# GpSimd's elementwise work of an attention and two-MoE kernel put on VectorE, and the ELU in another form

## The chip, the cores and the metric

One core of one Trainium2 chip runs the whole program. The metric is the device time in microseconds of one execution; three executions of the kernel before were timed. TensorE (PE), VectorE (DVE), ScalarE (ACT), GpSimd (POOL) and SyncE (SP, which issues the DMAs here) each work through a queue of their own in order.

## What is computed

Attention whose keys and values are means over 8 neighbouring positions, then an MoE with ELU, then a second MoE with a softmax-gated unit and a normalization. Everything is float32 in and out; 4608 tokens of 512 numbers.

```python
k_p = k.reshape(B, H, Sp, 8, D).mean(axis=3)          # v_p likewise; B, H, S, D = 8, 8, 576, 64
attn = softmax(scale * q @ k_p.T)                     # sums + 1e-9
x = (attn @ v_p) -> (4608, 512)
h = x @ w_in                                          # 512 -> 2048
g = np.where(h > 0, h, np.exp(np.minimum(h, 0)) - 1)  # ELU
x = g @ w_out                                         # 2048 -> 512
h = x @ w_in2                                         # 512 -> 1024
solu = h * softmax(h)
out = ((solu - mean) / sqrt(var + 1e-6) * g_ln) @ w_out2
```

## The kernel before

A float32 product is made of three fp32r products (high x high, high x low, low x high), so every operand is split: ScalarE casts the high part, VectorE or GpSimd subtracts it for the low part. Tokens come in 9 blocks of 512.

**Direct stage** (to about 410 us; blocks j = 0, 1, 2). For each block and each f of 16 column blocks of 128 hidden units, `m_h1` runs 12 matmuls into a PSUM bank `h` and ScalarE makes `e`; `m_elu` makes the ELU on VectorE and ScalarE's cast `gh`; `m_glo` the low part `gl_`; `m_o1` 12 matmuls into four banks `o`. Attention of later tokens runs in between, in pieces (`att_half`): scores on TensorE (L173), maximum and subtraction on VectorE (L189, L198), exponent on ScalarE (L203), sum on VectorE (L212 to L214), the division `es` on GpSimd (L216), transposes (L228, L233) with ScalarE copies `a`, products with v (L252) and copies `xr`, `xh`. `w_out_split` makes the high and low parts of w_out: `woh` on ScalarE, `wol` on GpSimd (L452).

While blocks 1 and 2 run, `combo_in` and `combo_out` prepare weight combinations for the rest: for each of 8 pairs of column blocks, `ci` (from w_in) and `co` (from w_out), each by `combos`: four subtractions of 128x256 (L469), two casts of 128x512 on ScalarE (L474), two low-part subtractions (L479), and DMAs to the DRAM tensors `w1d` and `w3d`. One generator hands these steps out, 2.6 of them per half column block.

**Paired stage** (about 412 to 961 us; three rounds of two blocks). Two blocks and the two halves of features form a 2x2 product that is done with seven products instead of eight (P1, P2, V, S2, S3, A22, S4). `h_step` runs the seven products of hidden pair k over combined operands, adds them up with `keep` (ScalarE copies a bank to `sp`, L670) and VectorE adds (L703, L714, L722), and applies `elu` to the four quarters `g` (11, 12, 21, 22) in SBUF. The quarter 21 comes straight from a bank (argument `h`, L680 to L682), the others from SBUF (`h` is None, L676 to L678). `g_sum` forms sums of quarters in place, 128x1024 each: V, S3 and S4 on GpSimd, S2 on VectorE (L736). `g_op` splits them (cast `op` L742, low part L743) for `mul_o`, which runs the second seven products against the streamed `wr` tiles. Attention for later blocks goes on in the first two rounds; in the last, `prep_in` prepares the second MoE's weights (L391 to L394, L422, L428, L429).

**MoE 2** (from 961 us) is TensorE work in a fixed rhythm: products x, y, z (L832), transposes (L904), products po (L919).

Most of the program isn't issued in the order written: a scheduler orders each engine's queue by its own cost estimates and the data dependences (only the start is under `manual_schedule`). So a change of engine also moves neighbouring instructions.

Of the kernel before, what the change touches and what calls it, by code (L numbers as in the profile page):

```python
# [9 lines left out]
F32R = mybir.dt.float32r  # L10
# [3 lines left out]
AF = mybir.ActivationFunctionType  # L14
ALU = mybir.AluOpType
# [4 lines left out]
def kernel(  # L20
# [15 lines left out]
    nc = tc.nc  # L36
# [428 lines left out]
    def combos(b11, b12, b21, b22, t, w, d):  # L465

        t1, t2, t3, t4 = (t[:, i] for i in range(4))
        for o, x, y in ((t1, b12, b11), (t3, b22, b12), (t2, b22, t1), (t4, b21, t2)):
            nc.gpsimd.tensor_tensor(o, x, y, op=ALU.subtract)  # L469
            yield  # L470
        tf = t.rearrange("p s a f -> p (s a f)")
        for m in range(2):
            c = slice(512 * m, 512 * m + 512)
            nc.scalar.copy(w.bitcast(F32R)[:, c], tf[:, c])  # L474
            yield
        for m in range(2):
            c = slice(512 * m, 512 * m + 512)
            eng = nc.vector if m else nc.gpsimd
            eng.tensor_tensor(tf.bitcast(F32R)[:, c], tf[:, c], w[:, c], op=ALU.subtract)  # L479
            yield  # L480
        for hl, z in enumerate((w, tf)):
            nc.sync.dma_start(out=d[hl], in_=z.rearrange("p (s f) -> p s f", s=4))
        yield
# [39 lines left out]
    def m_h1(j, f):  # L523
        n = sizes[j]
        g, fo = f // 4, (f % 4) * P
        h = ps.tile([P, 512], F32, name="h1", tag="B")
# [5 lines left out]
                )  # L532
                i += 1
        e = p1.tile([P, 512], F32, name="e", tag="e")
        if j == 0:

            nc.scalar.activation(e[:, 0:n], h[:, 0:n], AF.Relu, scale=-1.0)
            nc.scalar.activation(e[:, 0:n], e[:, 0:n], AF.Exp, scale=-1.0)
        else:
            nc.scalar.activation(e[:, 0:n], h[:, 0:n], AF.Exp)  # L540
        gt[j, f] = (e, h)

    def m_elu(j, f):
        n = sizes[j]
        e, h = gt[j, f]
        if j == 0:
            nc.vector.scalar_tensor_tensor(  # L547
                e[:, 0:n], e[:, 0:n], 1.0, h[:, 0:n], op0=ALU.subtract, op1=ALU.max
            )
        else:  # L550
            nc.vector.tensor_scalar(e[:, 0:n], e[:, 0:n], 1.0, 1.0, op0=ALU.min, op1=ALU.subtract)
            nc.vector.tensor_tensor(e[:, 0:n], e[:, 0:n], h[:, 0:n], op=ALU.max)
        gh = p1.tile([P, 512], F32R, name="gh", tag="gh")
        nc.scalar.copy(gh[:, 0:n], e[:, 0:n])  # L554
        gt[j, f] = (e, gh)
# [116 lines left out]

    def elu(d, h=None):
        e = pq.tile([P, 512], F32, name="ep", tag="ep", bufs=2)
        if h is None:
            nc.scalar.activation(e, d, AF.Exp)  # L676
            nc.vector.tensor_scalar(e, e, 1.0, 1.0, op0=ALU.min, op1=ALU.subtract)
            nc.vector.tensor_tensor(d, e, d, op=ALU.max)  # L678
        else:
            nc.scalar.activation(e, h, AF.Relu, scale=-1.0)  # L680
            nc.scalar.activation(e, e, AF.Exp, scale=-1.0)
            nc.vector.scalar_tensor_tensor(d, e, 1.0, h, op0=ALU.subtract, op1=ALU.max)  # L682

    hx = {}

# [40 lines left out]
    GQ = {"P1": 11, "P2": 12, "V": 21, "S2": 21, "S3": 11, "A22": 22, "S4": 12}  # L726

    def g_sum(n, t):
        d, x, y, op, eng = {
            "V": (21, 21, 22, ALU.add, nc.gpsimd),  # L730
            "S2": (21, 21, 11, ALU.subtract, nc.vector),
            "S3": (11, 22, 21, ALU.subtract, nc.gpsimd),
            "S4": (12, 12, 21, ALU.subtract, nc.gpsimd),
        }[n]
        d, x, y = (gslot(q, 2 * t, 2) for q in (d, x, y))
        eng.tensor_tensor(d, x, y, op=op)  # L736

    def g_op(s, t):
        n = ORDER[s]
# [558 lines left out]
```

## Time and profile before

| | us |
|---|---|
| median of the times (1375.02 to 1377.74) | 1376.96 |
| the profiled execution | 1375.29 |
| its span, first to last instruction | 1373.5 |
| PE busy in the span | 1290.4 (94%) |
| DVE busy | 1020.6 (74%) |
| ACT busy | 725.6 (53%) |
| POOL busy | 365.4 (27%) |

The span is that of one execution under the profiler. A share of busy time is a mean over stages with different limits, so it is read stage by stage: where TensorE is busy all the time at clock 1.00, nothing that another engine does costs time; where it isn't, its waits name what came last, and that engine's queue shows what stood ahead. The granted clock is a share of full speed (2.4 GHz). Matmuls overlap one another, so their pace is read from the distance of their starts and not from their durations.

### The profile page before, as it was taken

Reading aid. Unit: us, or ns where it says so; the run is one execution under the profiler, and the core shown is the slowest. Engines: PE = TensorE matmul, PEld = TensorE weight load, DVE = VectorE, ACT = ScalarE, POOL = GpSimd, SP = SyncE. Lnnn points to the kernel's source line nnn. Section 1 sums busy time; section 2 is a strip of 40 time slices with the busy share of each in tenths; the row PEclk is TensorE's granted clock in tenths of the full one; section 3 lists DMA queues with packets and bytes.
Section 4 is the critical chain, followed back from the end, with each engine's and each line's share of the span. In section 5 each row is a group of like instructions: output and inputs, shape, how many; then the busy total and the mean of one; then the engine's idle time right before and its main releaser. Section 6 shows DMA issues by size and latency. Waiting matters only on the chain.

```text
span 1373.5 us, 17423 instructions
## 1 busy us (share of the span) xinstructions
PE 1290.4 (94%) x5972; PEld 1023.6 (75%) x5972; DVE 1020.6 (74%) x1517; ACT 725.6 (53%) x1266; POOL 365.4 (27%) x266
## 2 busy tenths in 40 slices
PE   5889988899999999999999999899999999999998
PEld 4667766677876787777887767778788888888887
DVE  7888785776676889849799488996766666757573
ACT  4778553455454574445564346633545554545453
POOL 3546766752220216301126000170000000000000
PEclk8999998999999999999999999999999999999999
DMA  8588476683338775787765778899311011101001
GB/s 261 175 247 255 141 234 194 208 274 115 95 97 295 229 228 181 237 275 211 215 188 198 261 238 266 289 349 343 115 54 54 24 54 54 54 25 53 31 17 39
DMA packets 143273, 236.06 MB, mean 172 GB/s; under 512 B 13520, under 2 KB 61136, under 8 KB 141776
## 3 DMA queue, kind: packets, MB, share of 16 engines
q1 hardware_dynamic: 143184, 234.93, 53.1%
q8 instruction: 48, 0.79, 0.2%
q14 instruction: 41, 0.34, 0.1%
HBM read 168.82 MB, written 66.06 MB: 171 GB/s over the span
## 4 chain that ended last, share of the span: by engine, by line
PE 44%; DVE 8%; DMA 4%; ACT 2%; issue 1%; SPq 0%; POOL 0%; POOLq 0%; ACTq 0%; DVEq 0%
PE po L919 14%; PE oA L752 8%; PE x L832 7%; PE hA L658 5%; PE z L832 3%; DVE op L743 3%; PE pt L904 2%; PE y L832 2%; DMA raw<-in_w 2%; DMA x1d<-xo 1%; PE oB L752 1%; DMA wr<-w3d 1%; DVE g L736 1%; PE xyz L832 1%; DMA su<-x0d 1%
## 5 line engine op out<-in xcount | busy, mean ns | idle before, releaser
L752 PE MATMUL oA<-op,wr 128*128 128x512 f32 x864 | 206.5, 397 | 3.9 <-DMA wr<-w3d 3.3
L919 PE MATMUL po<-w,dhl 128*128 128x512 f32 x864 | 208.5, 394 | 0.9 <-ACT dhl L907 0.9
L752 PEld LDWEIGHTS oA<-op,wr 128*128 128x128 f32 x864 | 163.4, 191 | 43.8 <-issue 5.9
L919 PEld LDWEIGHTS po<-w,dhl 128*128 128x128 f32 x864 | 160.9, 188 | 35.4 <-ACT dhl L907 1.3
L736 POOL TENSOR_TENSOR g<-g,g 128x1024 f32<-128x1024 f32 x36 | 109.0, 3046 | 279.3 <-DVE g L682 231.2
L743 DVE TENSOR_TENSOR op<-g,op 128x1024 fp32r<-128x1024 f32 x84 | 136.9, 1654 | 21.1 <-ACT op L742 20.9
L742 ACT CAST op<-g 128x1024 fp32r<-128x1024 f32 x84 | 87.3, 1051 | 86.6 <-PE oA L752 40.0
L894 POOL TENSOR_TENSOR sc<-sc,mhalf 128x1 f32<-128x1 f32 x36 | 23.3, 646 | 402.5 <-DVE sc L893 327.2
L658 PE MATMUL hA<-sS,wr 128*128 128x512 f32 x432 | 111.7, 397 | 6.1 <-ACT sp L670 4.0
L452 POOL TENSOR_TENSOR wol<-wo,woh 128x512 fp32r<-128x512 f32 x48 | 72.9, 1519 | 108.1 <-ACT woh L451 108.0
L658 PEld LDWEIGHTS hA<-sS,wr 128*128 128x128 f32 x432 | 79.8, 189 | 28.8 <-ACT sp L670 6.9
L832 PE MATMUL x<-w,xh 128*128 128x512 f32 x272 | 97.4, 399 | 1.1 <-ACT sn L840 1.1
L882 DVE TENSOR_REDUCE sc<-hb 128x1 f32<-128x1024 f32 x18 | 21.9, 1219 | 94.9 <-ACT hb L868 94.3
L573 PE MATMUL o<-gh,woh 128*128 128x512 f32 x192 | 81.6, 425 | 2.8 <-ACT gh L554 2.8
L216 POOL TENSOR_TENSOR es<-es,sm 128x720 f32<-128x720 f32 x28 | 45.7, 1632 | 141.1 <-DVE sm L214 116.8
L573 PE MATMUL o<-gh,wol 128*128 128x512 f32 x192 | 79.0, 412 | 1.7 <-POOL wol L452 1.7
L530 PE MATMUL h<-xh,wh 128*128 128x512 f32 x192 | 78.6, 409 | 0.6 <-DVE e L547 0.6
L530 PE MATMUL h<-xh,wl 128*128 128x512 f32 x192 | 75.3, 392 | 0.5 <-POOL wl L375 0.5
L530 PE MATMUL h<-xl,wh 128*128 128x512 f32 x192 | 75.1, 391 | 0.0
L922 ACT ACTIVATE ot<-po,sc 128x512 f32<-128x512 f32 x36 | 24.6, 685 | 90.0 <-PE po L919 55.7
L228 PE MATMUL pt<-ident,es 128*72 128x128 f32 x256 | 41.2, 288 | 27.5 <-DVE es L198 9.1
L670 ACT COPY sp<-hA 128x512 f32<-128x512 f32 x72 | 41.7, 583 | 44.7 <-PE hA L658 44.6
(336 smaller groups left out, 2915.6 us busy)
## 6 DMA issues: line engine op xcount, KB each, us to landing
wr<-w1d SPq DMA_DIRECT2D x168, 256.0 KB
wr<-w3d SPq DMA_DIRECT2D x168, 256.0 KB
raw<-in_w SPq DMA_DIRECT2D x48, 512.0 KB
v<-in_v SPq DMA_DIRECT2D x32, 288.0 KB
x1r<-x1d SPq DMA_DIRECT2D x9, 1024.0 KB
out<-ot SPq DMA_DIRECT2D x36, 256.0 KB
w1d<-ci SPq DMA_DIRECT2D x16, 512.0 KB
w3d<-co SPq DMA_DIRECT2D x16, 512.0 KB
```

The costliest lines, as they stand in the source:

```text
L216: n = eng.tensor_tensor(es, es, bc(sm, NG), op=ALU.mult)
L452: nc.gpsimd.tensor_tensor(ol, t[:, f % 4, :], oh.bitcast(F32), op=ALU.subtract)
L530: nc.tensor.matmul(h[:, 0:n], a[g][:, kk, fo:fo + P], x[j][:, kk, 0:n], start=(i == 0), stop=(i == 3 * KDM - 1))
L573: nc.tensor.matmul(acc, a[:, dm * P:(dm + 1) * P], x[:, 0:n], start=(f == 0 and m == 0), stop=(f == NF - 1 and m == 2))
L658: nc.tensor.matmul(bank, w[:, a, kk], x[:, b, kk], start=(start and m == 0), stop=(stop and m == 5), skip_group_check=True,)
L670: nc.scalar.copy(t, bank)
L736: eng.tensor_tensor(d, x, y, op=op)
L742: nc.scalar.copy(o[:, 0], src)
L743: nc.vector.tensor_tensor(o[:, 1], src, o[:, 0].bitcast(F32), op=ALU.subtract)
L752: nc.tensor.matmul(banks[d], ws[i][:, a, d * P:(d + 1) * P], o[:, b, i], start=(start and t == 0 and i == 0 and m == 0), stop=(stop and t ...
L832: nc.tensor.matmul(bank, x[:, o:o + P], w[:, y + k, :], start=(start and m == 0), stop=(stop and m == 5), skip_group_check=True,)
L919: nc.tensor.matmul(po, a[:, c, :], w[c // 4][:, c % 4, :], start=(m == 0), stop=(m == 3 * NC2 - 1))
```

## The change

Three edits. `combos` issues all its subtractions on VectorE (before: the four L469 and one of the two L479 on GpSimd). `g_sum` issues all sums on VectorE (before: V, S3, S4 on GpSimd). The ELU is everywhere the form that block j = 0 and the quarter 21 had already: ScalarE's Relu of -h, then Exp of its negative, and one VectorE step max(e - 1, h); before, the other places had one ScalarE Exp of h and two VectorE steps (minimum with 1 and minus 1, then the maximum with h).

```diff
@@ combos
         for o, x, y in ((t1, b12, b11), (t3, b22, b12), (t2, b22, t1), (t4, b21, t2)):
-            nc.gpsimd.tensor_tensor(o, x, y, op=ALU.subtract)
+            nc.vector.tensor_tensor(o, x, y, op=ALU.subtract)
             yield
...
-            eng = nc.vector if m else nc.gpsimd
-            eng.tensor_tensor(tf.bitcast(F32R)[:, c], tf[:, c], w[:, c], op=ALU.subtract)
+            nc.vector.tensor_tensor(tf.bitcast(F32R)[:, c], tf[:, c], w[:, c], op=ALU.subtract)
@@ m_h1
-        if j == 0:
-
-            nc.scalar.activation(e[:, 0:n], h[:, 0:n], AF.Relu, scale=-1.0)
-            nc.scalar.activation(e[:, 0:n], e[:, 0:n], AF.Exp, scale=-1.0)
-        else:
-            nc.scalar.activation(e[:, 0:n], h[:, 0:n], AF.Exp)
+        nc.scalar.activation(e[:, 0:n], h[:, 0:n], AF.Relu, scale=-1.0)
+        nc.scalar.activation(e[:, 0:n], e[:, 0:n], AF.Exp, scale=-1.0)
@@ m_elu
-            nc.vector.tensor_scalar(e[:, 0:n], e[:, 0:n], 1.0, 1.0, op0=ALU.min, op1=ALU.subtract)
-            nc.vector.tensor_tensor(e[:, 0:n], e[:, 0:n], h[:, 0:n], op=ALU.max)
+        nc.vector.scalar_tensor_tensor(
+            e[:, 0:n], e[:, 0:n], 1.0, h[:, 0:n], op0=ALU.subtract, op1=ALU.max
+        )
@@ elu
-        if h is None:
-            nc.scalar.activation(e, d, AF.Exp)
-            nc.vector.tensor_scalar(e, e, 1.0, 1.0, op0=ALU.min, op1=ALU.subtract)
-            nc.vector.tensor_tensor(d, e, d, op=ALU.max)
-        else:
-            ...
+        h = d if h is None else h
+        nc.scalar.activation(e, h, AF.Relu, scale=-1.0)
+        nc.scalar.activation(e, e, AF.Exp, scale=-1.0)
+        nc.vector.scalar_tensor_tensor(d, e, 1.0, h, op0=ALU.subtract, op1=ALU.max)
@@ g_sum
-            "V": (21, 21, 22, ALU.add, nc.gpsimd),
-            "S2": (21, 21, 11, ALU.subtract, nc.vector),
-            "S3": (11, 22, 21, ALU.subtract, nc.gpsimd),
-            "S4": (12, 12, 21, ALU.subtract, nc.gpsimd),
+            "V": (21, 21, 22, ALU.add),
+            "S2": (21, 21, 11, ALU.subtract),
+            "S3": (11, 22, 21, ALU.subtract),
+            "S4": (12, 12, 21, ALU.subtract),
...
-        eng.tensor_tensor(d, x, y, op=op)
+        nc.vector.tensor_tensor(d, x, y, op=op)
```

What stands in the queues shows it best. VectorE's queue in block 1, around the ELU of one column block (`h_2105`; `gl_` is a low part of the activations, `xl` and `vr` are attention's), before:

```order
L493 TENSOR_TENSOR ci<-wh,wl 128x512
L551 TENSOR_SCALAR e<-e 128x512
L552 TENSOR_TENSOR e<-e,h_2105 128x512
L479 TENSOR_TENSOR ci<-ci 128x512
L561 TENSOR_TENSOR gl__2127<-e,gh 128x512
L479 TENSOR_TENSOR co<-co 128x512
L273 TENSOR_TENSOR xl_1511<-at,xh_1510 128x384
```

The same place in the changed kernel:

```order
L541 SCALAR_TENSOR_TENSOR e<-e,h_2105 128x512
L469 TENSOR_TENSOR ci<-ci 128x256 x3
L552 TENSOR_TENSOR gl__2127<-e,gh 128x512
L469 TENSOR_TENSOR ci<-ci 128x256
L478 TENSOR_TENSOR ci<-ci 128x512
L273 TENSOR_TENSOR xl_1511<-at,xh_1510 128x384
L157 TENSOR_REDUCE vr_2348<-v_2042 72x128
L478 TENSOR_TENSOR ci<-ci 128x512
L469 TENSOR_TENSOR co<-wo 128x256 x2
L469 TENSOR_TENSOR co<-wo,co 128x256 x2
```

The 256-wide subtractions stand between the ELU and its low part now, and the ELU is one row instead of two. GpSimd's queue in block 1, before:

```order
L216 TENSOR_TENSOR es_1479<-es_1479,sm_1514 128x720
L469 TENSOR_TENSOR co<-wo 128x256 x2
L469 TENSOR_TENSOR co<-wo,co 128x256 x2
L479 TENSOR_TENSOR co<-co 128x512
L452 TENSOR_TENSOR wol<-wo,woh 128x512
L469 TENSOR_TENSOR ci<-ci 128x256 x4
L479 TENSOR_TENSOR ci<-ci 128x512
L452 TENSOR_TENSOR wol<-wo,woh 128x512
```

And in the changed kernel, from the same division on:

```order
L216 TENSOR_TENSOR es_1480<-es_1480,sm_1514 128x720
L452 TENSOR_TENSOR wol<-wo,woh 128x512 x2
L216 TENSOR_TENSOR es_1661<-es_1661,sm_1722 128x720
L452 TENSOR_TENSOR wol<-wo,woh 128x512 x3
L216 TENSOR_TENSOR es_1870<-es_1870,sm_1903 128x720
```

Only divisions and weight remainders are left there. ScalarE's queue in the first half of a round of the paired stage (`ep` the ELU's temporary, `sp` a kept bank, `a` attention's), before:

```order
L676 ACTIVATE ep<-g_5931 128x512
L670 COPY sp<-hA 128x512 x3
L676 ACTIVATE ep<-g_5933 128x512
L229 COPY a_5970<-pt_1_6144 72x512
L676 ACTIVATE ep<-g_5930 128x512
L235 COPY a_5970<-pr_6150 72x2x64
L680 ACTIVATE ep<-hA 128x512
L681 ACTIVATE ep<-ep 128x512
```

The same place in the changed kernel:

```order
L667 ACTIVATE ep<-g_5931 128x512
L661 COPY sp<-hA 128x512
L668 ACTIVATE ep<-ep 128x512
L661 COPY sp<-hA 128x512 x2
L667 ACTIVATE ep<-g_5933 128x512
L229 COPY a_5970<-pt_1_6144 72x512
L668 ACTIVATE ep<-ep 128x512
L667 ACTIVATE ep<-g_5930 128x512
L235 COPY a_5970<-pr_6150 72x2x64
L668 ACTIVATE ep<-ep 128x512
```

Each ELU has a second activation, and two of the three copies `sp` stand behind one of them.

## Rows read from the trace of the kernel before

**Rows 1.** Busy by stage: stretch, length, PE, PEld, DVE, ACT, POOL (instructions), clock, DMA share, GB/s.

```profile
160.00:300.00 140.00, 116.72 (x545) 90.16 (x544) 102.77 (x144) 66.12 (x138) 102.21 (x96) 0.93 0.69 221
300.00:410.00 110.00, 109.79 (x557) 87.15 (x555) 76.92 (x117) 56.56 (x112) 28.84 (x22) 1.00 0.38 118
500.00:600.00 100.00, 94.53 (x456) 74.51 (x453) 86.69 (x94) 53.05 (x88) 36.28 (x13) 0.98 0.68 212
787.00:882.00 95.00, 86.25 (x341) 65.49 (x342) 83.84 (x131) 52.98 (x88) 8.21 (x3) 0.95 0.79 258
```

**Rows 2.** PE's waits, 200 to 250 us: who waited for whom, total, times, longest.

```profile
PE pt L228 <- DVE es L198: 5.0, 1, 5.0
```

**Rows 3.** ACT in order of time around 258 us: start, us, what, idle before and releaser.

```profile
258.50 0.62 ACT L474 CAST co<-co 128x512 fp32r<-128x512 f32 x1 [1.66 <-POOL co L469]
...
259.91 0.32 ACT L266 COPY xr<-at 128x192 f32<-128x192 f32 x1
```

**Rows 4.** PE in order of time behind that copy.

```profile
260.38 1.04 PE L228 MATMUL pt<-ident,es 128*72 128x128 f32 x4 [5.24 <-ACT xr L266]
...
262.07 0.63 PE L573 MATMUL o<-gl__2127,woh 128*128 128x512 f32 x1
262.50 0.63 PE L573 MATMUL o<-gh,woh 128*128 128x512 f32 x1
...
264.90 0.39 PE L573 MATMUL o<-gh,woh 128*128 128x512 f32 x1
265.13 0.39 PE L573 MATMUL o<-gh,wol 128*128 128x512 f32 x1
```

**Rows 5.** Groups of POOL, 150 to 300 us: line, shapes, count, busy, mean ns, idle before.

```profile
L452 POOL TENSOR_TENSOR wol<-wo,woh 128x512 fp32r<-128x512 f32 x18 | 25.6, 1423 | 23.2 <-ACT woh L451 23.1
L469 POOL TENSOR_TENSOR ci<-ci 128x256 f32<-128x256 f32 x28 | 24.6, 890 | 11.7 <-DVE ci L493 11.3
L469 POOL TENSOR_TENSOR co<-wo 128x256 f32<-128x256 f32 x16 | 16.3, 1038 | 1.4 <-DMA w3d<-co 1.3
L469 POOL TENSOR_TENSOR co<-wo,co 128x256 f32<-128x256 f32 x16 | 12.9, 803 | 0.5
L479 POOL TENSOR_TENSOR co<-co 128x512 fp32r<-128x512 f32 x8 | 10.6, 1326 | 0.5
L479 POOL TENSOR_TENSOR ci<-ci 128x512 fp32r<-128x512 f32 x7 | 10.4, 1484 | 0.4
L216 POOL TENSOR_TENSOR es<-es,sm 128x720 f32<-128x720 f32 x7 | 10.3, 1474 | 5.8 <-DVE sm L214 5.8
```

**Rows 6.** Groups of DVE, 150 to 300 us, in the same columns.

```profile
L552 DVE TENSOR_TENSOR e<-e,h 128x512 f32<-128x512 f32 x16 | 10.8, 678 | 0.2
L551 DVE TENSOR_SCALAR e<-e 128x512 f32<-128x512 f32 x16 | 10.5, 657 | 1.1 <-ACT e L540 1.1
...
L479 DVE TENSOR_TENSOR ci<-ci 128x512 fp32r<-128x512 f32 x7 | 8.6, 1232 | 14.4 <-ACT ci L474 14.4
...
L547 DVE SCALAR_TENSOR_TENSOR e<-e,h 128x512 f32<-128x512 f32 x1 | 0.7, 687 | 1.1 <-ACT e L538 1.1
```

**Rows 7.** Single lines over the whole span: count, ns least/median/most, first and last start.

```profile
L807 DVE TENSOR_TENSOR xs<-x1r x18: 414/416/427, 954.5 to 1314.4; 128x256 f32<-128x256 f32 x18
...
L736 DVE TENSOR_TENSOR g<-g,g x12: 1207/2527/3392, 530.3 to 915.1; 128x1024 f32<-128x1024 f32 x12
...
L677 DVE TENSOR_SCALAR ep<-ep x72: 409/420/2659, 431.4 to 886.4; 128x512 f32<-128x512 f32 x72
```

**Rows 8.** PE's waits, first 500 to 600 us, then 787 to 877 us.

```profile
PE pt L228 <- POOL es L216: 5.3, 2, 3.4
...
PE hA L658 <- ACT sp L670: 4.7, 5, 2.2
```

**Rows 9.** Groups of the page over the span: sums on POOL, ELU's Exp behind a Relu.

```profile
L736 POOL TENSOR_TENSOR g<-g,g 128x1024 f32<-128x1024 f32 x36 | 109.0, 3046 | 279.3 <-DVE g L682 231.2 <-DVE g L678 19.9 <-DVE g L736 18.9
...
L681 ACT ACTIVATE ep<-ep 128x512 f32<-128x512 f32 x24 | 15.2, 632 | 0.5
```

More of the change, by code (lines that the diff above doesn't have):

```diff
@@ L545, in m_elu @@
         e, h = gt[j, f]
[L546 to L549, printed above, removed]
-        else:
-            nc.vector.tensor_scalar(e[:, 0:n], e[:, 0:n], 1.0, 1.0, op0=ALU.min, op1=ALU.subtract)
-            nc.vector.tensor_tensor(e[:, 0:n], e[:, 0:n], h[:, 0:n], op=ALU.max)
+        nc.vector.scalar_tensor_tensor(
+            e[:, 0:n], e[:, 0:n], 1.0, h[:, 0:n], op0=ALU.subtract, op1=ALU.max
+        )
         gh = p1.tile([P, 512], F32R, name="gh", tag="gh")
@@ L674, in elu @@
         e = pq.tile([P, 512], F32, name="ep", tag="ep", bufs=2)
-        if h is None:
-            nc.scalar.activation(e, d, AF.Exp)
-            nc.vector.tensor_scalar(e, e, 1.0, 1.0, op0=ALU.min, op1=ALU.subtract)
-            nc.vector.tensor_tensor(d, e, d, op=ALU.max)
[L679 to L682, printed above, removed]
+        h = d if h is None else h
+        nc.scalar.activation(e, h, AF.Relu, scale=-1.0)
+        nc.scalar.activation(e, e, AF.Exp, scale=-1.0)
+        nc.vector.scalar_tensor_tensor(d, e, 1.0, h, op0=ALU.subtract, op1=ALU.max)
     hx = {}
@@ L728, in g_sum @@
     def g_sum(n, t):
-        d, x, y, op, eng = {
-            "V": (21, 21, 22, ALU.add, nc.gpsimd),
-            "S2": (21, 21, 11, ALU.subtract, nc.vector),
-            "S3": (11, 22, 21, ALU.subtract, nc.gpsimd),
-            "S4": (12, 12, 21, ALU.subtract, nc.gpsimd),
+        d, x, y, op = {
+            "V": (21, 21, 22, ALU.add),
+            "S2": (21, 21, 11, ALU.subtract),
+            "S3": (11, 22, 21, ALU.subtract),
+            "S4": (12, 12, 21, ALU.subtract),
         }[n]
         d, x, y = (gslot(q, 2 * t, 2) for q in (d, x, y))
-        eng.tensor_tensor(d, x, y, op=op)
+        nc.vector.tensor_tensor(d, x, y, op=op)
     def g_op(s, t):
```

## The prediction

> **What bounds the kernel now.** I read first the table of busy time by stage, then TensorE's waits, then the queues behind the longest of them. In the table [rows 1] the stretch 300 to 410 us is TensorE at its limit: 109.79 us busy of 110, clock 1.00. The stretch 160 to 300 does the same kind of work (token block 1 of the direct stage, where 300 to 410 is block 2, each with its share of attention), 545 recorded matmuls against 557, and takes 140 us: 116.72 busy, clock 0.93, GpSimd busy 102.21. At the later stretch's rate it would take 545 / 557 x 110 = 107.6 us, so it loses 32.4. That is the largest sum that the change can reach. Two smaller ones follow: 500 to 600 us (5.5 us of TensorE idle), and 787 to 882 us, where 341 matmuls at the full pace of 0.23 us each (the last pair in [rows 4]) would take 78 of the 95 us, a loss of 17. From 961 us on the code is the same.
>
> Where the 32.4 us go is read in the queues. TensorE's long waits there are for es from VectorE (5.0 us) and for ScalarE's copy xr (5.2 us) [rows 2, 4]. The second copy was not slow: it stood in ScalarE's queue behind a cast of a weight combination (co, line 474) that itself waited 1.66 us for GpSimd's subtraction [rows 3]. After each such stop TensorE runs its next matmuls at 0.43 us apart, then at 0.23 [rows 4]: the lower of its two levels, 1.2 against 2.4 GHz, right after 5 us of idling. So the combinations cost TensorE time not by their busy time but by standing in two in-order queues while GpSimd is late, and the stop is paid a second time at the low clock.
>
> **The change, part by part.** *Combinations to VectorE.* GpSimd spends 24.6 + 16.3 + 12.9 us on 60 subtractions of 128x256 and 10.6 + 10.4 us on 15 of 128x512 in this stretch, 74.8 in all [rows 5]. On VectorE the 256-wide form takes 0.416 us in MoE 2, where GpSimd is nearly idle [rows 7]: 60 x 0.416 = 25.0. The 512-wide form I price at 0.68, the ELU's maximum of that width [rows 6]: 15 x 0.68 = 10.2. The new ELU drops one VectorE step of 0.657 us in 16 column blocks, 10.5 us [rows 6]; its single step (687 ns) costs what the maximum did (678 ns) [rows 6]. VectorE's demand in the stretch becomes 102.8 + 25.0 + 10.2 - 10.5 = 127.5 us. Part of the 102.8 is VectorE held up by GpSimd: seven ci halves took 1.232 us [rows 6] where 0.68 is the free price, 3.9 us; with a little for the rest I take 5 off: 122.5 us. That is above TensorE's 107.6, so the bound moves to VectorE. How full can VectorE's queue be? Its fullest long stretches stand at 86.69 of 100 and 83.84 of 95, 88% [rows 1]; full would be 122.5. I take 93%, between the two: 131 us, **9 us less** than now. The ends: 107.6 us (-32) if VectorE fits beside TensorE, and 127.5 / 0.87 = 147 (+7) if nothing is freed and the queue fills no better than elsewhere. The extra ScalarE step, 16 x 0.63 us for the second activation [rows 9] = 10 us on 66.12 busy of 140 [rows 1], is hidden by ScalarE's idle half; without that cover it would be 10 us.
>
> As the order shows, ScalarE's casts now wait for VectorE's subtractions in place of GpSimd's. What is queued behind such a cast is as before (gh, woh, xr), but VectorE delivers its four subtractions in 4 x 0.416 = 1.7 us, where GpSimd's took 3.6 by the mean of the ci form [rows 5]. What is late next is VectorE's own queue: gl_ and the ELU step, for which TensorE's second products wait.
>
> *Sums of activations.* 36 sums cost GpSimd 109.0 us, 3.05 each [rows 9]; VectorE's shortest such sum is 1.207, its median 2.527 and its longest 3.392 while GpSimd works on others [rows 7]. With GpSimd free I take 1.21 for all 48: 36 x 1.21 = 43.6 us added, 12 x (2.53 - 1.21) = 16 saved at the median, and the stretch has room for it: VectorE loses the ELU step, 72 x 0.42 = 30 us at the median, up to 2.66 each [rows 7]. I put this at nothing by itself, since TensorE hides it; without the cover the difference of the three terms, nearly nothing, would be the price. What lies on the path in 500 to 600 us is two waits of TensorE, 5.3 us together, for the softmax division es, which stands in GpSimd's queue behind the sums [rows 8]. Those sums are gone from that queue: **6 us less** with the half clock behind the waits; ends 0 and 7.
>
> *ELU in 787 to 882 us.* VectorE is busy 83.84 of 95 us here [rows 1]. It loses 24 steps of 0.42 = 10.1, gains four sums of 1.21 = 4.8, and is no longer held up by GpSimd, 2.659 - 0.42 = 2.2 us at the worst step [rows 7]: about 76, 80%. ScalarE gains 24 x 0.632 = 15.2 [rows 9] on 52.98: 68 of 95. TensorE waits there for ScalarE's copy sp out of its bank, 4.7 us in five waits [rows 8], and that copy queues behind activations that wait for VectorE. A less loaded VectorE shortens this; a longer ScalarE chain lengthens it. The stretch's first 10 us (the operands' build behind a load) stay. Of 17 us lost I take **7 back**; ends 12 back, and 7 more lost (half of ScalarE's 15.2 us coming ahead of copies).
>
> Sum: 9 + 6 + 7 = 22 us less. The profiled execution took 1375.29 us (span 1373.5 and 1.8 around it): 1353.3. It lies 1.7 under the median of the runs shown, 1376.96, so **1355 us** on that footing, with 1345 to 1365 for this case.
>
> A page speaks against the Relu: the Trainium skill, "ScalarE: Activation LUTs", Rules for kernel authors, says to use VectorE and not ScalarE for relu and min. The rows agree on the price (0.42 against 0.632 us [rows 7, 9]); by it the change would lose 0.21 us per block wherever ScalarE were the fuller engine, which it is in no stage of the table.
>
> **The rivals.** *VectorE and GpSimd stand in each other's way in block 1* (slower). The weight remainders wol, 25.6 us, and divisions es, 10.3 us, stay on GpSimd [rows 5], and VectorE now has 60 more subtractions with both inputs in SBUF for them to meet. The rows show such meetings: 2.659 us for a step of 0.42, 3.392 for a sum of 1.21 [rows 7]. If all 36 us are added to VectorE's 127.5, block 1 takes 163 us, 23 more than now; with 13 saved later the kernel is 10 slower, 1387 us. It decides from 9.6 us a column block on ((140 + 13) / 16), against my 131 / 16 = 8.2. For it: block 1 has no spare VectorE time. Against it: GpSimd falls from 102 us busy to 36. The Trainium skill's page "SBUF — State Buffer", Who interferes with whom, states just this: a VectorE instruction with two SBUF inputs and a GpSimd instruction that reads SBUF exclude each other for a whole instruction; the trace agrees with it in the sum of 3.392 us, which has two such inputs. Chance 0.10.
>
> *VectorE fits* (TensorE becomes the bound in block 1): -32 - 13 = -45, 1332 us. For it, the contention that I kept may mostly go; against it, 122.5 us of work in 108. Chance 0.12.
>
> *ScalarE's chain takes the place of VectorE's* in 787 to 882: 7 more lost instead of 7 back, so -8, 1369 us. For it: TensorE's waits there already end on ScalarE [rows 8]. Against: ScalarE is 56% busy. Chance 0.14.
>
> *Nothing comes of it*: block 1 exchanges GpSimd's lateness for VectorE's, and the later gains go to transfers that end at the same time: 1377 us. Chance 0.10.
>
> **How the numbers follow.** The forecast has 0.54. A measurement of this kernel can tell about 0.2%, 2.8 us, from no change. Faster: 0.54 + 0.12 and nearly all of the ScalarE case, 0.78. Within: 0.12. Slower: 0.10. The range 1334 to 1380 leaves out the slower case and about half of the fastest.
>
> **What would show it.** In the changed profile: block 1 shorter by 5 to 15 us, GpSimd about 36 us busy in it, ScalarE's casts of ci and co no longer among the long waits, VectorE over 90% busy; sums at 1.21 us each, TensorE no longer waiting for es from GpSimd; in the last h stage fewer matmul waits for sp. It is wrong if TensorE in block 1 waits for gl_ and e as long as it waited for es and xr, if 256-wide subtractions take much over 0.42 us on VectorE, or if block 1 comes out at TensorE's 108 us.

## The result and the profile after

The changed kernel takes **1341.18 us** (median of four runs, 1339.62 to 1343.38) against 1376.91 of the kernel before on the same chip (1375.02 to 1377.74): ratio 0.9744, interval 0.9726 to 0.9761. It is 2.6% faster; the forecast was 1355, with 1334 to 1380 as range and 1345 to 1365 for its own case, which the time lies under.

To see where the time went, both traces are cut at the same landmarks: VectorE's ELU step that takes the maximum with `h`, in the first column block of blocks 0, 1 and 2 (the only step of the new form, the second of the old one), TensorE's first product of each round of the paired stage, and the first product of MoE 2. Lengths in us:

| | start | block 0 | block 1 | block 2 | round 1 | round 2 | round 3 | MoE 2 | span |
|---|---|---|---|---|---|---|---|---|---|
| before | 44.8 | 116.7 | 141.2 | 114.0 | 193.5 | 172.1 | 178.3 | 412.8 | 1373.5 |
| after | 47.5 | 120.0 | 122.4 | 115.3 | 183.0 | 169.9 | 171.5 | 411.9 | 1341.5 |

Block 1 gives 18.8 us, round 1 10.5, round 3 6.9, round 2 2.2. Block 0 pays 3.3 (the first combinations are made at its end) and block 2 1.3. The start, unchanged code, lies between 44.7 and 47.9 us over all the kernels of this study, so differences of 3 us there mean nothing.

The stages after, in the columns of [rows 1]: block 1 whole, then the stretches that answer to 500 to 600 and 787 to 882 us.

```profile
167.50:289.90 122.40, 114.07 (x570) 89.31 (x569) 117.27 (x199) 74.87 (x155) 38.82 (x22) 1.00 0.74 242
...
470.00:572.00 102.00, 101.87 (x503) 80.86 (x502) 91.48 (x114) 65.13 (x112) 9.27 (x5) 1.00 0.74 228
764.00:859.00 95.00, 89.20 (x373) 68.97 (x373) 78.03 (x119) 71.78 (x122) 0.00 (x0) 0.99 0.85 283
```

In block 1 GpSimd (fifth number) fell from 102 us to 39, VectorE (third) rose to 117.27 of 122.40, and the granted clock is 1.00 where it was 0.93; TensorE's longest wait there is 1.9 us now and was 5.2. In the stretch of round 1 TensorE is busy all the time.

The long waits of TensorE in block 1 [rows 2, 4] have shrunk (165 to 290 us: who waited for whom, total, times, longest):

```profile
PE pt L228 <- DVE es L198: 2.4, 2, 1.9
PE pt L228 <- ACT xr L266: 2.2, 2, 1.5
PE o L564 <- DVE gl__2206 L552: 1.5, 1, 1.5
```

ScalarE's casts, which waited for GpSimd before [rows 3], wait for VectorE now, 1.7 us at most for `co` and still 3.8 for `ci`. Before (161.5 to 302.7 us) and after:

```profile
ACT ci L474 <- POOL ci L469: 21.8, 10, 4.1
ACT co L474 <- POOL co L469: 17.3, 11, 3.5
...
ACT co L474 <- DVE co L469: 13.2, 11, 1.7
ACT ci L474 <- DVE ci L469: 12.2, 7, 3.8
```

What the moved work costs on VectorE in block 1 (groups: count, busy, mean ns of one, idle before), and what is left on GpSimd:

```profile
L469 DVE TENSOR_TENSOR ci<-ci 128x256 f32<-128x256 f32 x28 | 13.8, 521 | 0.0
L478 DVE TENSOR_TENSOR ci<-ci 128x512 fp32r<-128x512 f32 x14 | 13.2, 956 | 0.2
...
L478 DVE TENSOR_TENSOR co<-co 128x512 fp32r<-128x512 f32 x14 | 10.3, 760 | 0.2
```

```profile
L452 POOL TENSOR_TENSOR wol<-wo,woh 128x512 fp32r<-128x512 f32 x16 | 29.8, 1862 | 68.8 <-ACT woh L451 68.8
L216 POOL TENSOR_TENSOR es<-es,sm 128x720 f32<-128x720 f32 x6 | 9.1, 1512 | 15.1 <-DVE sm L214 15.1
```

The 256-wide subtraction takes 521 ns and not 416 [rows 7], the 512-wide 760 to 956 and not 680. GpSimd's remainder `wol` got slower, from 1423 ns [rows 5] to 1862, with less around it on its own engine. Both engines lengthen each other; the single instructions show it (count: least, median, most ns, first and last start; then rows in order of time: start and length in us):

```profile
L478 DVE TENSOR_TENSOR ci<-ci x14: 673/680/1774, 180.5 to 288.5; 128x512 fp32r<-128x512 f32 x14
...
285.45 1.50 POOL L452 TENSOR_TENSOR wol<-wo,woh 128x512 fp32r<-128x512 f32 x1 [1.88 <-ACT woh L451]
285.72 1.77 DVE L478 TENSOR_TENSOR ci<-ci 128x512 fp32r<-128x512 f32 x1
...
207.12 4.98 POOL L452 TENSOR_TENSOR wol<-wo,woh 128x512 fp32r<-128x512 f32 x1 [4.99 <-ACT woh L451]
207.46 1.28 DVE L478 TENSOR_TENSOR co<-co 128x512 fp32r<-128x512 f32 x2
208.66 1.28 DVE L492 TENSOR_TENSOR ci<-wh,wl 128x512 f32<-128x512 f32 x2
```

The first two rows are a VectorE step and the GpSimd instruction it meets: the step starts while `wol` runs and ends 0.54 us after `wol` does (287.49 and 286.95). In the last three it is GpSimd that stands, 4.98 us for one `wol`, while VectorE runs steps with two inputs in SBUF without a gap. Every lengthened VectorE step of block 1 is of the first kind. Counting those that take over 0.15 us more than the fastest tenth of their form, there are 36 before, 23.9 us over in all, and 18 after, 18.4 us over. Each one starts while a GpSimd instruction runs and ends 0.03, 0.28 or 0.55 us behind it. So in block 1 only 5.5 us of this time came back, because more VectorE steps meet fewer GpSimd instructions.

Over the whole span, the low part `op` before, then after it `op`, the sums in front of it and the new ELU step:

```profile
L743 DVE TENSOR_TENSOR op<-g,op 128x1024 fp32r<-128x1024 f32 x84 | 136.9, 1654 | 21.1 <-ACT op L742 20.9
...
L730 DVE TENSOR_TENSOR op<-g,op 128x1024 fp32r<-128x1024 f32 x84 | 102.6, 1234 | 32.9 <-ACT op L729 32.8
...
L669 DVE SCALAR_TENSOR_TENSOR g<-ep,g 128x512 f32<-128x512 f32 x72 | 50.0, 705 | 25.8 <-ACT ep L668 25.7
L723 DVE TENSOR_TENSOR g<-g,g 128x1024 f32<-128x1024 f32 x48 | 60.8, 1291 | 0.1
```

48 sums at 1291 ns take 60.8 us of VectorE; before, 12 sums of VectorE and 36 of GpSimd took 27.5 and 109.0 [rows 9 for the second]. VectorE's `op`, which the change doesn't touch, took 136.9 us before (1654 ns each) and takes 102.6 now; with the sums alone moved (experiment 1) it is 106.2, so most of these 34 us had been GpSimd's sums.

### The profile page after: what moved, and what is told of

It reads as the page before. It is cut to its first block, busy times and chain, and to the rows that moved or that the text cites. A ratio compares the mean times of both kernels' runs of the same rounds, so it can differ in the third digit from the quotient of the medians.

```text
span 1341.5 us, 17404 instructions
## 1 busy us (share of the span) xinstructions
PE 1278.1 (95%) x5972; PEld 1017.6 (76%) x5972; DVE 988.0 (74%) x1529; ACT 778.7 (58%) x1370; POOL 185.8 (14%) x150
## 4 chain that ended last, share of the span: by engine, by line
PE 64%; DVE 7%; DMA 6%; ACT 2%; issue 2%; POOL 0%; SPq 0%; POOLq 0%; DVEq 0%; ACTq 0%
PE po L906 14%; PE hA L649 12%; PE oA L739 11%; PE x L819 7%; PE z L819 3%; PE o L564 2%; PE pt L891 2%; PE h L529 2%; PE hB L649 2%; PE oB L739 2%; PE y L819 2%; DMA raw<-in_w 1%; PE at L252 1%; PE at L173 1%; DMA x1d<-xo 1%
## 5 line engine op out<-in xcount | busy, mean ns | idle before, releaser
L730 DVE TENSOR_TENSOR op<-g,op 128x1024 fp32r<-128x1024 f32 x84 | 102.6, 1234 | 32.9 <-ACT op L729 32.8
L452 POOL TENSOR_TENSOR wol<-wo,woh 128x512 fp32r<-128x512 f32 x48 | 81.3, 1694 | 172.1 <-ACT woh L451 172.0
L669 DVE SCALAR_TENSOR_TENSOR g<-ep,g 128x512 f32<-128x512 f32 x72 | 50.0, 705 | 25.8 <-ACT ep L668 25.7
L723 DVE TENSOR_TENSOR g<-g,g 128x1024 f32<-128x1024 f32 x48 | 60.8, 1291 | 0.1
L819 PEld LDWEIGHTS x<-w,xh 128*128 128x128 f32 x272 | 51.1, 188 | 12.6 <-ACT sn L827 1.8
```

What stands on the lines that cost most here:

```text
L452: nc.gpsimd.tensor_tensor(ol, t[:, f % 4, :], oh.bitcast(F32), op=ALU.subtract)
L723: nc.vector.tensor_tensor(d, x, y, op=op)
L730: nc.vector.tensor_tensor(o[:, 1], src, o[:, 0].bitcast(F32), op=ALU.subtract)
L819: nc.tensor.matmul(bank, x[:, o:o + P], w[:, y + k, :], start=(start and m == 0), stop=(stop and m == 5), skip_group_check=True,)
```

## The experiments

The theory was that of the prediction: combinations on the slow GpSimd make ScalarE's and VectorE's in-order queues stand, and the new price is VectorE's amount of work. The main rival: GpSimd's and VectorE's instructions lengthen each other, wherever they stand. The kernels below are in the order in which they answer. All lengths are by the landmarks of the table; medians are of four runs (ten for the ELU alone and for the old kernel with its combinations spread).

**1. Each part alone.** The combinations alone (the two lines of `combos`, the rest as before):

> The kernel before with only the weight combinations moved to VectorE; sums and ELU as before. Block 1 is the time from the ELU of its first column block to that of block 2's first: 141.2 us before, 122.4 in the changed kernel. Queue theory (ScalarE and VectorE stood behind GpSimd's late subtractions): block 1 becomes bound by VectorE, whose load is the changed kernel's 117 us plus the 10 us of the old ELU step, so about 128 to 130 us; the paired rounds stay; about 1364 us. Rival, load theory (only VectorE's amount of work counts): VectorE gets 35 us more work in block 1 and gives none up, so block 1 is 147 us or longer and the kernel 1383 us or more.

Measured: 1356.69 us, ratio 0.9861 (0.9836 to 0.9886). Block 1 is 121.5 us, 19.7 shorter: the gain of block 1 comes from this part whole, and the old ELU on VectorE doesn't lengthen it, where the queue theory expected 128 to 130 us. The step that the new ELU drops costs little once GpSimd's combinations are gone, 415 ns where it was 657 [rows 6]:

```profile
L550 DVE TENSOR_SCALAR e<-e 128x512 f32<-128x512 f32 x16 | 6.6, 415 | 0.0
...
164.50:286.10 121.60, 114.28 (x563) 89.51 (x562) 120.31 (x216) 65.50 (x138) 43.17 (x22) 0.99 0.75 244
```

VectorE is busy for 120.31 of 121.60 us, 99%.

The sums alone (the table in `g_sum`):

> The kernel before with only the sums of activations moved to VectorE. Queue theory: blocks 0 to 2 as before; rounds 1, 2 and 3 (193.5, 172.1, 178.4 us before; 183.0, 169.9, 171.5 in the changed kernel) give most of round 1's 10 us and 2 to 4 of round 3, because the divisions no longer queue behind sums on GpSimd: about 1364 us. Rival (the ELU is what shortened the rounds): no more than 4 us gained, 1373 us or more. Every sum takes 1.2 to 1.3 us under both.

Measured: 1358.47 us, 0.9868 (0.9846 to 0.989). Round 1 is 7.0 us shorter and round 3 8.7. In round 1 TensorE's waits for the division `es`, 5.3 us [rows 8], are 0.8, which is 4.5 of the 7.0 us:

```profile
PE pt L228 <- POOL es L216: 0.8, 1, 0.8
```

Round 3 before, and with the sums moved (columns of [rows 1]):

```profile
782.30:960.70 178.40, 163.70 (x674) 128.48 (x673) 152.06 (x184) 89.02 (x132) 37.21 (x12) 0.96 0.86 298
```

```profile
774.40:944.10 169.70, 158.71 (x673) 123.79 (x672) 141.49 (x196) 89.61 (x132) 0.00 (x0) 1.00 0.88 306
```

VectorE has 12 instructions more and is 10.6 us less busy: the steps that GpSimd's sums had lengthened, 24.5 us over by the count above, are gone.

The ELU alone:

> The kernel before with only the ELU's form changed (Relu and Exp on ScalarE, one VectorE step). Queue theory: block 1 stays near 141 us because GpSimd's combinations are as late as before; rounds gain 5 to 7 us in round 3: about 1370 us. Load theory: VectorE loses 10 us in block 1 and 30 to 40 us in the rounds, block 1 about 131 us, rounds 10 us less: about 1357 us.

Measured: 1372.78 us, 0.9976 (0.996 to 0.9993), a gain of 0.1 to 0.4%. Block 1 stays at 139.2 us, as the queue theory had it. Round 1 gains 5.1 us, block 2 loses 3.7, round 3 loses 1.5.

Both others with the old ELU:

> The changed kernel with the old ELU back. Queue theory with VectorE as block 1's new bound: block 1 goes from 122.4 to about 130 us and round 3 gives 3 to 5 us back, about 1354 us. Rival (the ELU is worth nothing where ScalarE takes what VectorE loses): 1341 to 1344 us.

Measured: 1339.97 us, 0.9732 (0.9711 to 0.9753), the same as the changed kernel's 0.9744 within the intervals. On top of the other parts the new ELU gives 4.0 in round 1 and 1.0 in round 2, and takes 3.4 in round 3, 2.3 in block 2 and 0.9 in block 1. In round 3 TensorE's first products of `mul_o` then wait longer for a weight transfer; with the new ELU

```profile
PE oA L739 <- DMA wr<-w3d: 3.2, 1, 3.2
```

and with the old one

```profile
PE oA L751 <- DMA wr<-w3d: 1.2, 2, 0.8
```

Over the study that wait is 3.0 to 6.6 us in the seven kernels with the new ELU in round 3, 0.2 to 1.8 in five with the old one, but 3.3 and 4.0 in the other two with the old one. What makes the transfer land late was not found, and a stage of one profile varies: round 3 came out 4.0 us shorter with the combinations alone, which don't touch it. So the 3.4 us can't be told from chance, nor can the 4.0 of round 1, which came out between 182.8 and 189.1 us in kernels with the same code there (experiments 4 and 7); that the ELU gives nothing on top of the other parts rests on the two times.

**2. Is it the queues that wait for GpSimd?** Kernel before, with a combination's casts and both low parts on GpSimd too:

```diff
-            nc.scalar.copy(w.bitcast(F32R)[:, c], tf[:, c])
+            nc.gpsimd.tensor_copy(w.bitcast(F32R)[:, c], tf[:, c])
...
-            eng = nc.vector if m else nc.gpsimd
-            eng.tensor_tensor(tf.bitcast(F32R)[:, c], tf[:, c], w[:, c], op=ALU.subtract)
+            nc.gpsimd.tensor_tensor(tf.bitcast(F32R)[:, c], tf[:, c], w[:, c], op=ALU.subtract)
```

> The kernel before with the weight combinations entirely on GpSimd: its four subtractions, both casts (ScalarE's before) and both low parts (one was VectorE's). No in-order queue but GpSimd's own then contains a step that waits for a combination; VectorE and ScalarE lose work in block 1, GpSimd gains about 16 casts and 16 subtractions of 128x512, some 40 us. Theory of the prediction (a cast or a subtraction in ScalarE's and VectorE's queues that waits for the late GpSimd holds up what stands behind it): block 1 falls from 141 us to 121 or less, though GpSimd is busier, and the kernel gains 15 us or more, unless GpSimd then hands the weights out too late for the first round. Rival (VectorE's and GpSimd's steps lengthen each other, and this holds TensorE up): with more GpSimd work block 1 stays at 141 us or gets longer, 1377 us or more.

Measured: 1389.39 us, 1.0096 (1.0062 to 1.0131), block 1 at 145.7. By the letter the rival wins, but my premise that no queue but GpSimd's own waits for a combination was false. VectorE still makes the first step of `ci` (the sum of `wh` and `wl`), and that now stands in VectorE's queue until the buffer of an earlier `ci` is written out:

```profile
DVE ci L492 <- DMA w1d<-ci: 25.9, 5, 8.4
```

So a late GpSimd holds the other queues through buffers as well as through operands. TensorE also waits for GpSimd's late divisions `es`, 4.2 us in block 1 and 5.1 in block 2. The run decides nothing between the two.

**3. Is it VectorE's amount of work in block 1?** Changed kernel, each combination step not issued ahead of the newest ELU step at its place in the program, so that the combinations spread over blocks 1 and 2:

```diff
-                next(todo, None)
+                with tc.issue_after(gate["elu"]):
+                    next(todo, None)
```

(`gate["elu"]` holds the last ELU instruction of `m_elu`.)

> The changed kernel with one more rule: each step of the weight combinations may not be issued ahead of the newest ELU step of VectorE at the place where the program hands it out, so that the combinations spread over blocks 1 and 2 and don't gather in block 1. Theory (VectorE's amount of work sets block 1's 122 us: busy 117 of 122 there, 68 of 107 in block 2): block 1 falls to 109 to 113 us, block 2 gains at most 3, about 1331 us. Rival (block 1 is long for another reason, such as the order of the steps within a column block or GpSimd's weight remainders): block 1 stays at 120 us or more, 1338 to 1344 us.

Measured: 1328.92 us, 0.9662 (0.9632 to 0.9691). Block 1 is 110.7 us, block 2 117.2, as the theory has it.

```profile
160.90:271.60 110.70, 110.34 (x557) 87.61 (x556) 95.58 (x155) 69.08 (x142) 33.57 (x22) 1.00 0.67 214
```

**4. Or what GpSimd does beside it?** Changed kernel without the spread, block 1's remainders `wol` on VectorE too:

```diff
-        nc.gpsimd.tensor_tensor(ol, t[:, f % 4, :], oh.bitcast(F32), op=ALU.subtract)
+        (nc.vector if keep else nc.gpsimd).tensor_tensor(
+            ol, t[:, f % 4, :], oh.bitcast(F32), op=ALU.subtract
+        )
```

> The changed kernel with the weight remainders wol of block 1 on VectorE too, so that only the divisions es are left on GpSimd in block 1. VectorE gains 16 steps of about 0.68 us, 11 us, in a stretch where it is 96% busy. If VectorE's amount of work sets block 1: 122 + 11 less what collisions with GpSimd had cost it, 125 to 133 us, and 1345 to 1352 us in all. If the collisions with GpSimd's remainders (1.86 us each now, 1.42 before) were what holds VectorE: block 1 at 120 us or less, under 1340 us.

Measured: 1336.2 us, 0.9704 (0.9679 to 0.9729). Block 1 is 113.0 us, under the 120 that spoke for the rival:

```profile
167.00:280.00 113.00, 113.00 (x574) 90.21 (x573) 110.32 (x201) 72.27 (x150) 10.49 (x7) 1.00 0.74 242
```

VectorE has 201 instructions instead of 199, with 15 remainders among them (some combinations went to block 2), and is busy 7 us *less*, in part because 13 other steps left the block; TensorE never idles beside a VectorE that is 98% busy. The 512-wide subtractions are back at their free price, and no long one is among them (lines are two further down here):

```profile
L480 DVE TENSOR_TENSOR co<-co x12: 627/683/693, 171.2 to 264.6; 128x512 fp32r<-128x512 f32 x12
L480 DVE TENSOR_TENSOR ci<-ci x12: 672/678/693, 180.3 to 278.4; 128x512 fp32r<-128x512 f32 x12
```

So both are true of the 122 us: VectorE was full, and part of what filled it, 18.4 us, was what GpSimd lengthened its steps by. Either less work in that stretch (3) or no GpSimd beside it (4) brings block 1 to TensorE's own length.

**5. Would spreading have done without the change of engine?** Kernel before, with the spread of (3) alone:

> The kernel before, nothing moved to another engine, with the one rule of the spread kernel: combination steps not ahead of the newest ELU step at the place where the program hands them out. GpSimd's 75 us of combinations then lie in two blocks instead of one. If block 1 was long because combinations gathered there and GpSimd was late with them: block 1 at 112 to 120 us, block 2 up to 6 longer, about 1355 us, and the change of engine would have been one of two ways to the same end. If GpSimd's and VectorE's steps in each other's way held it (the same number of meetings, only spread over more time): the sum of blocks 1 and 2 stays near the 255 us of before, block 1 at 125 or more, 1365 us or more.

Measured: 1375.36 us, 0.997 (0.9951 to 0.9989). By the times it gains 0.1 to 0.5%; the profiled execution is the slowest of the ten, 4.4 us over the median. In it block 1 falls to 130.5 us, block 2 rises to 125.6: 256.1 together, 255.2 before, the numbers that were expected of the rival. Spreading alone moves the loss; the engine must change. And yet neither VectorE nor GpSimd is full:

```profile
162.10:292.60 130.50, 119.30 (x560) 93.26 (x560) 85.58 (x132) 60.44 (x126) 65.71 (x60) 0.93 0.56 180
```

What stops TensorE there can be followed in order of time (start, us, what, idle before and releaser). GpSimd from 219.95 us:

```profile
219.95 1.12 POOL L469 TENSOR_TENSOR ci<-ci 128x256 f32<-128x256 f32 x1 [0.63 <-DVE ci L493]
221.03 1.73 POOL L452 TENSOR_TENSOR wol<-wo,woh 128x512 fp32r<-128x512 f32 x1
222.73 2.24 POOL L469 TENSOR_TENSOR ci<-ci 128x256 f32<-128x256 f32 x3
225.05 1.29 POOL L479 TENSOR_TENSOR ci<-ci 128x512 fp32r<-128x512 f32 x1
226.29 1.43 POOL L469 TENSOR_TENSOR co<-wo 128x256 f32<-128x256 f32 x2
227.68 1.55 POOL L469 TENSOR_TENSOR co<-wo,co 128x256 f32<-128x256 f32 x2
```

ScalarE, whose casts wait for them with the ELU's Exp (L540) and the copy `a` (L229) behind:

```profile
224.19 0.62 ACT L474 CAST ci<-ci 128x512 fp32r<-128x512 f32 x1 [3.51 <-POOL ci L469]
225.00 0.63 ACT L474 CAST ci<-ci 128x512 fp32r<-128x512 f32 x1 [0.20 <-POOL ci L469]
228.45 0.62 ACT L474 CAST co<-co 128x512 fp32r<-128x512 f32 x1 [2.82 <-DMA w1d<-ci]
228.97 0.59 ACT L540 ACTIVATE e<-h 128x512 f32<-128x512 f32 x1
...
232.65 0.57 ACT L229 COPY a<-pt 72x512 f32<-72x512 f32 x1
```

VectorE and then TensorE:

```profile
229.60 1.25 DVE L551 TENSOR_SCALAR e<-e 128x512 f32<-128x512 f32 x1 [6.39 <-ACT e L540]
```

```profile
233.28 1.32 PE L173 MATMUL at<-kpbd,q 128*128 128x144 f32 x4 [3.58 <-ACT a L229]
```

The cast `co` at 228.45 starts when the first of the two subtractions in GpSimd's last row ends (227.68 + 1.55 / 2 = 228.46), whose result it casts; the transfer that its row names as releaser is beside the point. This is the mechanism of [rows 3], three engines long: GpSimd is behind by a few instructions, ScalarE stands for 3.51 and 2.82 us, VectorE for 6.39, TensorE for 3.58.

Is it this waiting, or VectorE's lengthened steps, that makes the block long? The mixture of experiment 7 has the same spread and the same old ELU in this block, with the combinations on VectorE:

```profile
162.30:274.70 112.40, 110.45 (x556) 87.33 (x556) 104.43 (x172) 59.24 (x125) 33.47 (x22) 1.00 0.66 212
```

The waits of ScalarE's casts in the old kernel with its combinations spread:

```profile
ACT co L474 <- POOL co L469: 9.9, 4, 4.3
...
ACT ci L474 <- POOL ci L469: 5.2, 4, 3.5
```

In the mixture VectorE is busy 18.9 us more and its steps are lengthened by 18.8 us in place of 13.5, and yet the old kernel's block 1 is 18 us longer. What it has and the mixture hasn't is ScalarE's casts waiting for GpSimd, 15.1 us in all. So what makes this block long is the waiting for GpSimd's results, and neither VectorE's amount of work nor its lengthened steps; how much of GpSimd's lateness VectorE causes in turn is open.

**6. GpSimd's instructions without anybody waiting for them.** Spread kernel (3), with GpSimd doing as many subtractions as before, into a tile that nobody reads (`extra` is true in blocks 1 and 2):

```diff
         nc.gpsimd.tensor_tensor(ol, t[:, f % 4, :], oh.bitcast(F32), op=ALU.subtract)
+        if extra:
+            z = ol.bitcast(F32)
+            for n in (256, 256, 448)[:2 + f % 2]:
+                nc.gpsimd.tensor_tensor(idle[:, 0:n], z[:, 0:n], z[:, 512 - n:512], op=ALU.subtract)
```

> The spread kernel, combinations on VectorE, but GpSimd does as many subtractions beside them as it did in the kernel before: behind each weight remainder of blocks 1 and 2 two of 128x256 and, behind every other one, one of 128x448 (the width that space was left for), from wol into a tile that nobody reads. 64 and 16 of them, some 70 us, about 35 us a block. No engine waits for their results; only GpSimd's own divisions and remainders stand behind them. The kernel before with its combinations spread had blocks 1 and 2 at 256 us together, the spread kernel 228. If steps of GpSimd and VectorE in each other's way cost the 28 us: 245 us or more for the two blocks, 1346 us or more in all. If the waiting of ScalarE's and VectorE's queues for GpSimd's results cost them: 228 to 234 us, 1329 to 1335 us.

Measured: 1348.46 us, 0.9788 (0.9759 to 0.9816): some 17 us more than the spread kernel by the ratios. In the profiled executions (here the slowest of the four, there the fastest) blocks 1 and 2 take 248.4 us, 20.5 more than the spread kernel's 227.9: 5.8 in block 1, 14.7 in block 2. Block 1:

```profile
160.40:276.90 116.50, 112.13 (x557) 88.70 (x556) 104.68 (x155) 68.91 (x143) 70.14 (x62) 0.99 0.64 204
```

With the same 155 instructions VectorE is busy 104.68 us instead of 95.58: 36.6 us more of GpSimd's work cost VectorE 9.1 us; its lengthened steps, by the count above, are 24.3 us over here and 15.3 there, which is all of it. The 256-wide `ci` steps took 566 ns in the spread kernel and take 705 here:

```profile
L474 DVE TENSOR_TENSOR ci<-ci 128x256 f32<-128x256 f32 x16 | 11.0, 705 | 0.0
```

In block 2 GpSimd's own queue adds to it: a division `es` is late and TensorE stands 3.6 us for it:

```profile
PE pt L229 <- POOL es L217: 3.6, 1, 3.6
```

So instructions of GpSimd whose results nobody needs cost TensorE 17 to 20 us in two blocks, part of it through the divisions behind them. VectorE carries more here (105 us busy) than in the old kernel with its combinations spread (86), so these can't simply be taken as that share of the old kernel's loss. Block 1 says more: its VectorE steps are lengthened as much as in the kernel before (24.3 and 23.9 us), with VectorE as busy (104.7 and 102.3), and it is 116.5 us long where that was 141.2.

**7. Towards a better kernel.** First a mixture: combinations and sums moved, combinations spread, new ELU in rounds 1 and 2 only.

> A candidate put together from the single parts: combinations and sums on VectorE, the combinations held to the program's place as in the spread kernel, the new ELU only in rounds 1 and 2 of the paired stage, the old one in blocks 1 and 2 of the direct stage and in the last round. If the parts add up: 1340 (combinations and sums with the old ELU everywhere) less 5 (the ELU in rounds 1 and 2) less 10 (block 1 no longer bound by VectorE), about 1326 us. If block 1 isn't bound by VectorE's amount of work: about 1336 us. If the ELU's gain in rounds 1 and 2 came only from taking it out of the direct stage's neighbourhood: 1340 us.

Measured: 1330.61 us, 0.9655 (0.9617 to 0.9694), no better than the spread kernel (0.9662). Block 1 is 112.4 and block 2 118.8, each 1.6 to 1.7 longer, round 3 is the same (170.0 and 170.2): with VectorE's load spread, no difference shows from which ELU stands where.

Spread and block 1's remainders on VectorE:

> The spread kernel with block 1's weight remainders wol on VectorE too. Both kernels alone bring block 1 to 111 to 113 us, near TensorE's own 108. If they take away the same loss, as the theory of one bound in block 1 says: block 1 at 108 to 111 us, 1326 to 1330 us in all. If each took away a loss of its own: 1323 us or less. If VectorE, 96 us busy in the spread block 1, is then too full: block 1 over 112 us.

Measured: 1329.6 us, 0.9635 (0.9612 to 0.9657), block 1 at 110.0: the two remove the same loss, as expected of one bound. All three blocks' remainders on VectorE (`nc.vector` for `nc.gpsimd` without the condition of (4)):

> As the kernel before this one, with the weight remainders of all three blocks on VectorE (16 more in block 0, 16 in block 2), so that GpSimd does hardly more than the softmax divisions. If GpSimd's remainders still cost VectorE time in blocks 0 and 2: block 0 and block 2 each 2 to 4 us shorter, about 1322 us. If VectorE has no room there (block 0 is VectorE's fullest stage beside block 1): block 0 up to 5 us longer, 1332 us.

Measured: **1323.82 us**, 0.9597 (0.9581 to 0.9614), the best of the study and 1.5% under the changed kernel (0.9597 / 0.9744 = 0.985). Block 0 is 112.2 (115.5 with the spread alone), block 2 112.9 (117.2). Its block 1:

```profile
156.90:266.90 110.00, 110.00 (x557) 87.82 (x557) 95.14 (x172) 69.48 (x142) 9.63 (x6) 1.00 0.68 217
```

Against the spread kernel VectorE has 17 instructions more, 16 of them remainders, and is as busy (95.14 and 95.58): the 24 us that left GpSimd came to VectorE at no net time at all. Its lengthened steps fall from 15.3 us over to 5.2, which pays for nearly all of the 10.9 us that the 16 remainders take.

## Why the prediction was right, and where it wasn't

The direction and the place held: most of the time came out of block 1, then out of the sums. The time came out 14 us under the forecast, inside the range but under the 1345 to 1365 that I gave the forecast's case.

*Block 1, 9 us forecast, 18.8 measured* (15.5 with what block 0 pays). The mis-sized step is VectorE's fill of 93%, put between the fullest stretches of [rows 1] and full (122.5 / 0.93 is 131.7, so even by that step 8 us and not 9). The fullest stretch seen is no limit: VectorE ran at 117.27 of 122.40 (96%) in the changed kernel, 99% with the combinations alone, and 98% beside a TensorE that never idled. The demand was also smaller, 117.3 us for my 122.5, although the 57 subtractions of 128x256 took 28.9 us for the 23.7 that 0.416 each would make: without a deduction my sum was 127.5, so VectorE's other steps came out 127.5 - 117.3 + 5.2 = 15 us under it, not the 5 that I took off. The 16 low parts `gl_`, 1222 ns each before and 773 now, are 7 of these; some 6 are the overlap of the records of steps without a gap between them, which busy time counts once. The ELU step that I counted as 10.5 us saved here was not needed: block 1 was 121.5 us with the old ELU, whose step then took 6.6 us; the rest of the 10.5 was GpSimd's lengthening and went with the combinations.

*The rival that VectorE fits, 1332 us,* was nearer than the chance of 0.12 says: 1341 is between it and the forecast. What kept block 1 from it, as the runs with `wol` moved or the combinations spread show, was the remaining GpSimd work beside a VectorE with no room.

*The rival of collisions, 1387 us,* had a true mechanism at a wrong price. I let all 36 us left on GpSimd be added to VectorE's time; the run with idle subtractions shows 9.1 us for 36.6, a quarter (in experiment 7, 24 us taken off GpSimd gave 10.1 back), and the block got shorter all the same, since ScalarE's casts no longer waited for GpSimd. The Trainium skill's page "SBUF — State Buffer", Who interferes with whom, says that a VectorE instruction with two SBUF inputs and a GpSimd instruction that reads SBUF exclude each other for a whole instruction; the 680 ns step that took 1774 and the remainder that went from 1423 to 1862 ns agree with it.

*The queue theory* is seen in time order (experiment 5), and the comparison there bears it out for block 1: with VectorE's steps lengthened less and VectorE less busy, the block that waits for GpSimd is 18 us longer. The run meant to decide it (2) had a waiting step left in VectorE's queue and decides nothing, and (6) shows that 17 to 20 us can also be lost with nobody waiting for GpSimd's combinations. I named both mechanisms and treated the second as a rival to the change; in the rounds it was also much of what the change took away (24.5 us of VectorE's time in round 3, nothing left after).

*Sums, 6 us forecast,* 7.0 in round 1 with the sums alone, through the path named: `es` out from behind the sums. Their price of 1.21 us on VectorE was 1.29. I put round 2 at nothing; it gained 2.2. In round 3 I counted the sums as a cost of 4.8 us of VectorE; by themselves they brought 8.7 us there.

*ELU in round 3, 7 us forecast, 6.9 measured:* the right number for the wrong reason, by luck. The sums alone bring 8.7 us there, and the ELU alone none (round 3 was 1.5 longer). The step that failed is the one that gave those 7 us to a VectorE relieved of one ELU step. It was GpSimd's sums that had held VectorE and ScalarE's casts; the ELU by itself is worth 0.1 to 0.4%, and nothing on top of the other parts. TensorE's waits for `sp` stayed, 4.3 us for 4.7 [rows 8]. *ScalarE's chain*, the rival to which I gave 0.14, didn't show: these waits got no longer, and the 7 us that it would have cost are twice the 3.4 that might be its share. (The stretch had three sums on GpSimd, not the four that I added there; at 1.21 us that changes little.)

*The extra ScalarE step in block 1 at nothing:* 0.9 us between the new ELU and the old one there, in one profile each, which can't be told from nothing.

Of the signs that I named, GpSimd's 39 us in block 1, VectorE over 90% busy and the end of TensorE's waits for `es` came as said. Block 1 gained more than the 5 to 15 us, `ci` casts still waited up to 3.8 us and the waits for `sp` got no fewer. The 256-wide subtractions at 521 ns for 0.42 are a sign of being wrong that half came, and they show the rival's mechanism.

## What to carry to other kernels

In this kernel GpSimd's elementwise instructions on SBUF were paid for on both engines: before costing a move to VectorE by adding its instructions' free price, look at what VectorE's unchanged instructions take more than their shortest time, because that can come back. What GpSimd makes late can cost more than what it lengthens: look for casts and subtractions in other queues that wait for its results, and at what stands behind them. A stretch in which one engine is over 95% busy is not yet at a limit: first see whether its instructions have their free length, then whether the work needs to stand in that stretch at all. And when parts of a change are predicted one by one, run them one by one; a total can be right with two terms at the wrong address.

## What the runs showed of the hardware that was not expected

- An engine's share can stand at 98% without holding another up: VectorE 110.32 of 113.00 us busy while TensorE was busy for all 113.00 of them at clock 1.00.
- Moving 16 remainders of 128x512 from GpSimd (1.57 us each beside the spread combinations) to VectorE (0.68 each in the kernel that had only block 1's moved) left VectorE's busy time in block 1 the same, 95.58 and 95.14 us.
- The GpSimd instruction pays too: `wol` took 1423 ns beside the old mix, 1862 beside a full VectorE (one of them 4.98 us), 1565 when VectorE's work was spread, 1498 in experiment 6.
- 36.6 us of GpSimd subtractions that nobody waits for cost VectorE 9.1 us in one block; in two blocks such subtractions cost the kernel 17 us by the ratios, 20.5 us in the profiled executions.
- Not every VectorE step is lengthened. In block 1 of the fourteen kernels, none of the 55 ELU maxima (one input in PSUM) and none of the reductions that started while a GpSimd instruction ran was over by more than 0.15 us; of the 80 low parts `gl_` (both inputs in SBUF) 67 were, and of the 45 steps `e<-e` (one input, in SBUF) 34.
